# Channel products on all 128 rows, with only their tails on half-row tiles, in the last stage of a convolution and spectral-mixing kernel

## The chip, the cores and the metric

The kernel runs on one core of a Trainium2 chip. The metric is the device time of one execution in microseconds, the median over several executions; lower is better. The engines are named as the profile names them: PE (TensorE's matmuls), PEld (TensorE's weight loads), DVE (VectorE), ACT (ScalarE), POOL (GpSimd) and SP (SyncE, which here only issues transfers). A product below is one matmul together with the load of its weights.

## What is computed

The input x is 8 x 3264 x 192. First every head (24 channels) is filtered along the sequence by 7 softmaxed taps. Then 64 Fourier modes of the result are mixed by complex 192 x 192 matrices and transformed back, and a gated residual is added:

```
x   = causal 7-tap convolution of the input, taps = softmax(weight) per head
X   = rfft(x, axis=1)[:, :64]
Yr  = Xr @ w_r - Xi @ w_i;   Yi = Xr @ w_i + Xi @ w_r      (per mode)
y   = irfft(Y, n=3264, axis=1)
u   = x + y
out = u + relu(u @ w_ch)                                   (float32)
```

## The kernel before, in words

The sequence of 3264 is cut into 25 tiles of 128 positions and one half tile of 64 positions. Batches go in pairs q = 0 to 3, so a slot `xall[:, slot(q, t), i, :]` holds 128 positions x 192 channels of batch 2q + i in bf16.

**First stage.** `conv` filters a unit of 4 or 5 tiles with 64 x 64 matmuls (line 285). `dft_unit` (line 311) multiplies the tiles by the table `ftab` of cosines and sines, and `cm_bank` and `ct_bank` (lines 360, 371) transpose the filtered tiles: `cm` has the first 128 channels on the 128 rows, `ct` the last 64 channels of batch 2q on rows 0 to 63 and of batch 2q + 1 on rows 64 to 127. `mix` (line 428) multiplies the modes by the weights, which POOL loads from DRAM in 32 transfers; this is where the kernel waits for the last of them.

**Second stage**, the one that is changed. Its unit is a double tile, `duo`: two slots, so four batch tiles of 128 x 192, collected in a double PSUM bank `zt` (128 x 2 x 512 float32, four of them, `za0`, `za1`, `zb2`, `zb3`, taken in turn). The list `duos` holds 50 plain double tiles, one of the four half tiles (marked "h"), and two entries (the integers 2 and 3) at which the mixed modes of two more batches are prepared (`zw_batch`, `zw_copy`). For a double tile there are three kinds of product:

- `c`: channels by `w_ch`, 192 columns each. Per batch tile a part with the first 128 channels (`cm` and `wm`) and a part with the last 64 channels (`ct` and `wt2`, the tail).
- `g`: the inverse transform of the spectrum times `w_ch` (`ftab` and `zw`, first half), 384 columns, one per slot. After `c` and `g`, ACT applies the relu in place (line 521).
- `y`: the inverse transform of the spectrum itself (`ftab` and `zw`, second half), 384 columns, one per slot, added on top after the relu. Then `finish` adds x on DVE (line 540) into one of 7 output buffers and SP issues the transfer to DRAM (line 549, or 554 in the first four).

Before the change every product of this stage is cut into two halves of the rows: `both` (line 485) issues the product's rows 0 to 63 for one slot of the double tile and rows 64 to 127 for the other, right behind each other, as two row tiles of TensorE that run at the same time on different banks. With `first` = 0 the lower rows serve slot 0 and the upper rows slot 1; with `first` = 1 they change places. All matmuls of it are at line 499. Since two row tiles may not add into one bank at once, `turn` (line 245) puts a wait for the last matmuls of one arrangement ahead of the first matmul of the other. The order of the work is written out by hand in the loop at line 596: for entry n, `c` and `g` in the first arrangement, the second half of `y` of n - 2 and its `finish`, then `c` and `g` of n in the second arrangement, the relu, and the first half of `y` of n - 1. `first_c` (line 564) does the `c` products of the first two double tiles earlier, between the last `mix` calls.

Of the kernel before, what the change touches and what calls it, by code (L numbers as in the profile page):

```python
# [9 lines left out]
ALU = mybir.AluOpType  # L10
# [9 lines left out]
def kernel(  # L20
# [9 lines left out]
    nc = tc.nc  # L30
    B, S, D = x.shape
# [5 lines left out]
    P = 128  # L37
    NQ = B // 2
    NF = S // P
# [13 lines left out]
    def sb(name, shape, dtype, **kw):  # L53
        return pool.tile([P] + shape, dtype, tag=name, name=name, **kw)


    xall = sb("xall", [NSLOT, 2, D], BF16, align_bytes=256)
# [7 lines left out]
    cm, ct = cc[:, :, 0:CB - NT, :], cc[:, :, CB - NT:CB, :]  # L65
    ftab = sb("ftab", [NT + 1, 2 * MODES], BF16)
# [5 lines left out]
    zw = mixa[:, 0:2 * B * D].rearrange("p (b t d) -> p b t d", b=B, t=2)  # L72
    band = sb("band", [H, 2 * P], BF16)
    wm = sb("wm", [2 * D], BF16)
    w1 = sb("w1", [2 * D], BF16)
    wt2 = sb("wt2", [D], BF16)
# [54 lines left out]
    def slot(q, t):  # L131
        return NT * q + t

    def load_unit(q, t0, n, only=None):
        nf = min(n, NF - t0)
        s0 = slot(q, t0) + 1
        for i in range(2) if only is None else (only,):
# [7 lines left out]
                                           ap=[[0, P], [KK, H], [1, KK]]))  # L145
# [17 lines left out]
    for k in range(KK):  # L163
# [4 lines left out]
                            in1=wmax.unsqueeze(2).to_broadcast([P, H, KK]), op=ALU.subtract)  # L168
# [14 lines left out]
    for g in range(4):  # L183
        dst, srcv = band[32 * g:32 * g + 32, :, 32 * g:32 * g + PW], pk3[32 * g:32 * g + 32, :, :]
# [34 lines left out]
    for i in range(2):  # L219
        src = bass.AP(tensor=x.tensor, offset=x.offset + (i * S + P * NF) * D,  # L220
                      ap=[[D, HALF], [2 * S * D, NQ], [1, D]])
# [23 lines left out]
    def turn(names):  # L245

        nop = nc.tensor.nop()
        for name in names:
            tc.add_manual_dep(nop.ins, name, mybir.DependencyInfo(mybir.DependencyClass.Sync,
                                                                  mybir.DependencyReason.DATA),  # L250
                              reason="row tiles take turns on a bank")
# [144 lines left out]
    for k, u in enumerate(units):  # L396
# [5 lines left out]
        if k:  # L402
            q, t0, n = units[k - 1]
# [52 lines left out]
    some(2)  # L456


    def z_pieces(u, row, which):

        r = slice(64 * row, 64 * row + 64)
        res = []
        if u[0] == "h":
            for k, q in enumerate(u[1]):
                cols = slice(D * k, D * k + D)
                if which == "c":
                    res.append((cols, cm[r, q, 2 * NF, :], wm[r, 0:D]))
                    res.append((cols, ct[r, q, NF, :], wt2[r, :]))
                else:
                    for i in range(2):  # L470
                        res.append((cols, ftab[r, NF + i, :], zw[r, 2 * q + i, 0 if which == "g" else 1, :]))
        else:
            q, t = u
            if which == "c":
                for i in range(2):
                    res.append((slice(D * i, D * i + D), cm[r, q, 2 * t + i, :], wm[r, 0:D]))
                res.append((slice(D * row, D * row + D), ct[r, q, t, :], wt2[r, :]))
            else:
                res.append((slice(0, 2 * D), ftab[r, t, :],
                            zw[r, 2 * q:2 * q + 2, 0 if which == "g" else 1, :]))  # L480
        return res

    held = {}

    def both(duo, zt, first, which, begin=False, end=False):


        lists = (z_pieces(duo[first], 0, which), z_pieces(duo[1 - first], 1, which))
        old = held.get(id(zt))
        if old is not None and old[0] != first and not begin:  # L490
            turn(old[1])
        last = [None, None]
        for k in range(max(len(lists[0]), len(lists[1]))):
            for row in range(2):
                lst, bank = lists[row], first ^ row
                if k >= len(lst):
                    continue
                cols, l, r = lst[k]
                mm = nc.tensor.matmul(zt[:, bank, cols], l, r, start=(begin and k == 0),  # L499
                                      stop=(end and k == len(lst) - 1), skip_group_check=True)  # L500
                last[row] = mm.ins.name
        held[id(zt)] = (first, last)

    def zw_batch(b, zt, k):
        nc.tensor.matmul(zt[:, k, 0:2 * D], yet[:, 0, :, b], wm[:], start=True, stop=False)
        nc.tensor.matmul(zt[:, k, 0:2 * D], yet[:, 1, :, b], w1[:], start=False, stop=True)

    def zw_copy(b, n, src, act):
        dst = zw[:, b:b + n, :, :].rearrange("p b t d -> p b (t d)")
        if act:  # L510
            nc.scalar.activation(out=dst, in_=src, func=ACT.Copy, scale=ascale[:, 0:1])
        else:
            nc.vector.tensor_scalar(out=dst, in0=src, scalar1=ascale[:, 0:1], scalar2=None, op0=ALU.mult)

    duos = [((q, t), (q, t + 1)) for q in range(2) for t in (0, 2)]
# [4 lines left out]
    def relu(zt):  # L520
        nc.scalar.activation(out=zt[:, :, 0:2 * D], in_=zt[:, :, 0:2 * D], func=ACT.Relu)  # L521

    def finish(n):
        duo, zt = items[n]
        o = outs[n % NO]
        if duo[0][0] == "h":
            for i in range(2):
                r = slice(HALF * i, HALF * i + HALF)
                nc.vector.tensor_tensor(out=o[r, :, :].rearrange("p k (a d) -> p k a d", a=2),  # L529
                                        in0=zt[r, :, 0:2 * D].rearrange("p k (a d) -> p k a d", a=2),  # L530
                                        in1=xall[r, NF:NF + NT * (NQ - 1) + 1:NT, i, :].rearrange(
                                            "p (k a) d -> p k a d", k=2), op=ALU.add)
            for i in range(2):
                r = slice(HALF * i, HALF * i + HALF)
                dst = bass.AP(tensor=out.tensor, offset=out.offset + (i * S + P * NF) * D,
                              ap=[[D, HALF], [2 * S * D, NQ], [1, D]])
                nc.sync.dma_start(out=dst, in_=o[r, :, :].rearrange("p k (a d) -> p (k a) d", a=2))
            return
        s = [slot(*u) for u in duo]
        nc.vector.tensor_tensor(out=o[:, :, :], in0=zt[:, :, 0:2 * D],  # L540
                                in1=xall[:, s[0]:s[1] + 1:s[1] - s[0], :, :].rearrange("p k i d -> p k (i d)"),
                                op=ALU.add)
        (q0, t0), (q1, t1) = duo
        ov = o[:, :, :].rearrange("p k (i d) -> p (k i) d", i=2)
        if t0 == t1:

            dst = bass.AP(tensor=out.tensor, offset=out.offset + (2 * q0 * S + P * t0) * D,
                          ap=[[D, P], [S * D, 4], [1, D]])
            nc.sync.dma_start(out=dst, in_=ov)
        else:  # L550
            for i in range(2):
                dst = bass.AP(tensor=out.tensor, offset=out.offset + ((2 * q0 + i) * S + P * t0) * D,
                              ap=[[D, P], [P * D, 2], [1, D]])
                nc.sync.dma_start(out=dst, in_=ov[:, i:4:2, :])

    N = len(duos)
    items = [[duo, None] for duo in duos]
# [4 lines left out]
                item[1] = Z[k % 4]  # L562

    def first_c(n):
        for first in range(2):
            both(*items[n], first, "c", begin=(first == 0))

    for g in range(NG):
        mix(g)
# [23 lines left out]
    assign({k: pp.tile([P, 2, 512], F32, tag=f"zb{k}", name=f"zb{k}") for k in (2, 3)})  # L593

    ahead = 2
    for n in range(N + 2):
        duo, zt = items[n] if n < N else (None, None)
        old = [items[n - k][0] if 0 <= n - k < N else None for k in range(3)]
        zq = isinstance(duo, int)
        if n < N:  # L600
            if zq:
                for i in range(2):
                    zw_batch(2 * duo + i, zt, i)
                zw_copy(2 * duo, 2, zt[:, :, 0:2 * D], True)
            else:
                if n >= ahead:
                    both(duo, zt, 0, "c", begin=True)
                both(duo, zt, 0, "g")
        if isinstance(old[2], tuple):
            both(*items[n - 2], 1, "y", end=True)  # L610
            finish(n - 2)
        if n < N and not zq:
            if n >= ahead:
                both(duo, zt, 1, "c")
            both(duo, zt, 1, "g")
            relu(zt)
        if isinstance(old[1], tuple):
            both(*items[n - 1], 0, "y")


# [28 lines left out]
```

## Time and profile before

| what | value |
|---|---|
| median of the runs | 190.3 us (190.28, 190.3 and 192.6) |
| the profiled execution | 191.59 us, span 189.7 us |
| instructions | 6202 |
| PE, PEld, DVE, ACT, POOL busy | 154.9, 102.3, 116.5, 94.2, 66.6 us |
| moved by DMA | 40.07 MB, of which 20.05 MB written |
| matmuls of the second stage (line 499) | 33% of the span, 63 us, in the chain that ended last |

The span runs from the first to the last instruction of the profiled execution; 1.9 us of the execution's time lie outside of it. A row of the timeline or of the groups names the line, the engine, the operation, what it writes and reads, the part of TensorE's array that it uses (64\*128 is 64 rows by 128 columns), the shape of the data, and a count. The duration of a matmul is its latency; since matmuls are pipelined, what one costs is read from the distance between the starts of two neighbours, not from its duration.

### The profile page before, as it was taken

The page shows a single profiled execution, that of the slowest core. Times are in us where ns is not written, and L with a number is a line of the kernel's source. Part 1 is how long each engine was busy: PE and PEld are TensorE (multiplying, and loading weights), DVE is VectorE, ACT ScalarE, POOL GpSimd, SP SyncE. Part 2 cuts the span into 40 slices and gives each one's busy share as a digit, 9 for nine tenths or more (in the row PEclk, how much of TensorE's full clock was granted, in tenths as well). Part 3 has the DMA queues.
Part 4 walks back from the last instruction along what each step waited for, and adds up shares of the span by engine and source line. Part 5 has one row for each costly group of instructions (what it writes and reads, how often), then busy time and mean ns, then how long its engine had stood idle before and what let it go on. Part 6 is the DMA issues. An engine that isn't in the chain of part 4 may idle for free.

```text
span 189.7 us, 6202 instructions
## 1 busy us (share of the span) xinstructions
PE 154.9 (82%) x2687; PEld 102.3 (54%) x2687; DVE 116.5 (61%) x178; ACT 94.2 (50%) x129; POOL 66.6 (35%) x115
## 2 busy tenths in 40 slices
PE   0046579999999999898739749999999999999950
PEld 0023347766666756665427423666667566666620
DVE  4879555686677757464413302678575977777770
ACT  2066745545653553444523215566665666666630
POOL 7998899669557734105731000000000000000000
PEclk9999978999999999999985975999999999999997
DMA  5999999999999999995999920489986799999993
GB/s 55 147 188 189 190 173 178 191 191 192 189 190 178 178 203 207 206 207 81 199 196 205 206 46 0 152 271 363 304 274 223 225 362 323 328 325 324 327 327 133
DMA packets 63179, 40.07 MB, mean 211 GB/s; under 512 B 28848, under 2 KB 63152, under 8 KB 63152
## 3 DMA queue, kind: packets, MB, share of 16 engines
q0 software_dynamic: 36000, 19.59, 76.0%
q1 hardware_dynamic: 27152, 20.09, 31.7%
q8 instruction: 21, 0.34, 0.7%
q14 instruction: 6, 0.05, 0.1%
HBM read 39.20 MB, written 20.05 MB: 312 GB/s over the span
## 4 chain that ended last, share of the span: by engine, by line
PE 67%; DMA 13%; POOL 7%; issue 4%; DVE 4%; ACT 2%; POOLq 0%; DVEq 0%; ACTq 0%
PE zb L499 17%; PE za L499 16%; PE z L285 11%; PE low L311 9%; DMA arena<-in_moe_w_i_dram 6%; DMA arena<-in_moe_w_r_dram 4%; PE low L360 4%; POOL xall L140 4%; DMA xall<-in_x_dram 3%; PE low L371 3%; POOL arena L417 1%; PE low L324 1%; PE low L428 1%; DVE xall L305 1%; ACT za L521 1%
## 5 line engine op out<-in xcount | busy, mean ns | idle before, releaser
L285 PE MATMUL z<-xall,band 64*64 64x192 bf16 (+2 forms) x800 | 27.2, 265 | 17.5 <-DVE band L188 11.6
L140 POOL DMA_DIRECT2D xall<-in_x_dram x48 | 38.2, 810 | 7.0 <-DMA xall<-in_x_dram 5.0
L499 PEld LDWEIGHTS <-cc 64*128 64x128 bf16 x616 | 24.4, 94 | 21.2 <-PE za L499 7.3
L499 PE MATMUL za<-mixa,ftab 64*128 64x384 bf16 x208 | 32.7, 331 | 0.6 <-ACT za L521 0.3
L305 DVE CAST xall<-z 128x768 bf16<-128x768 f32 (+1 forms) x24 | 24.5, 1021 | 13.6 <-PE z L285 12.1
L540 DVE TENSOR_TENSOR arena<-za,xall 128x768 f32<-128x768 f32 x26 | 24.8, 956 | 10.8 <-PE za L499 4.5
L285 PEld LDWEIGHTS <-band 64*64 64x64 bf16 x800 | 18.1, 110 | 24.5 <-ACT band L186 12.0
L499 PE MATMUL zb<-mixa,ftab 64*128 64x384 bf16 (+1 forms) x224 | 31.2, 311 | 0.1
L303 ACT CAST xall<-z 128x768 bf16<-128x768 f32 (+1 forms) x24 | 20.4, 851 | 15.1 <-PE z L285 13.8
L540 DVE TENSOR_TENSOR arena<-zb,xall 128x768 f32<-128x768 f32 x24 | 22.9, 957 | 7.5 <-ACT za L521 4.0
L521 ACT ACTIVATE za<-za 128x768 f32<-128x768 f32 x26 | 20.7, 795 | 11.1 <-PE za L499 11.1
L521 ACT ACTIVATE zb<-zb 128x768 f32<-128x768 f32 x25 | 19.9, 795 | 12.3 <-PE zb L499 12.3
L499 PEld LDWEIGHTS <-ftab 64*128 64x128 bf16 x432 | 19.6, 94 | 4.2 <-issue 2.1
L311 PE MATMUL low<-xall,ftab 128*128 128x384 bf16 x100 | 21.6, 343 | 0.0
L499 PE MATMUL za<-wm,cc 64*128 64x192 bf16 x208 | 17.4, 245 | 0.2
L499 PE MATMUL zb<-wm,cc 64*128 64x192 bf16 x200 | 17.1, 248 | 0.4 <-DVE arena L529 0.3
L360 PEld LDWEIGHTS <-xall 128*128 128x128 bf16 x208 | 14.0, 103 | 3.2 <-issue 0.5
L340 DVE COPY cc<-low 128x1024 bf16<-128x1024 bf16 (+2 forms) x19 | 11.8, 620 | 4.4 <-PE low L360 2.3
L340 DVE COPY cc<-r 128x1024 bf16<-128x1024 bf16 (+2 forms) x10 | 6.0, 604 | 13.7 <-PE r L371 8.3
L338 ACT COPY cc<-low 128x1024 bf16<-128x1024 bf16 (+1 forms) x9 | 8.5, 941 | 11.4 <-PE low L371 5.1
L417 POOL DMA_DIRECT2D arena<-in_moe_w_r_dram x12 | 7.6, 632 | 17.1 <-PE low L428 10.4
L499 PE MATMUL za<-wt,cc 64*128 64x192 bf16 x104 | 12.8, 243 | 0.0
(104 smaller groups left out, 175.0 us busy)
## 6 DMA issues: line engine op xcount, KB each, us to landing
out_dram<-arena SPq DMA_DIRECT2D x46, 384.0 KB, 3.9
xall<-in_x_dram POOLq DMA_DIRECT2D x24, 192.0 KB, 8.1
xall<-in_x_dram POOLq DMA_DIRECT2D x16, 240.0 KB, 7.1
arena<-in_moe_w_r_dram POOLq DMA_DIRECT2D x12, 288.0 KB, 11.1
arena<-in_moe_w_i_dram POOLq DMA_DIRECT2D x12, 288.0 KB, 11.2
out_dram<-arena SPq DMA_DIRECT2D x10, 192.0 KB, 2.9
xall<-in_x_dram POOLq DMA_DIRECT2D x8, 144.0 KB, 7.0
cc<-in_moe_w_r_dram POOLq DMA_DIRECT2D x4, 288.0 KB, 7.2
```

Source lines behind the costliest of these rows:

```text
L140: nc.gpsimd.dma_start(out=xall[:, s0:s0 + nf, i, :], in_=src)
L285: mm = nc.tensor.matmul(ov[c], band[r, h, c.start + shift + 64 * (r is UP and c is LO): c.start + shift + 64 * (r is UP and c is LO) + 64] ...
L303: nc.scalar.copy(out=dst, in_=srcv)
L305: nc.vector.tensor_copy(out=dst, in_=srcv)
L311: nc.tensor.matmul(xp, ftab[:, t, :], xall[:, slot(q, t), :, :], start=(t == 0), stop=False, skip_group_check=True)
L338: nc.scalar.copy(out=out, in_=in_)
L340: nc.vector.tensor_copy(out=out, in_=in_)
L360: nc.tensor.transpose(tp[:, P * k:P * k + P], xall[:, slot(q, t), i, 0:P], ident[:])
L417: nc.gpsimd.dma_start(out=wbuf(g)[64 * half:64 * half + 64, :, :, :], in_=src[4 * g:4 * g + 4, :, :].rearrange("m (p j) e -> p m j e", j=3))
L499: mm = nc.tensor.matmul(zt[:, bank, cols], l, r, start=(begin and k == 0), stop=(end and k == len(lst) - 1), skip_group_check=True)
L521: nc.scalar.activation(out=zt[:, :, 0:2 * D], in_=zt[:, :, 0:2 * D], func=ACT.Relu)
L540: nc.vector.tensor_tensor(out=o[:, :, :], in0=zt[:, :, 0:2 * D], in1=xall[:, s[0]:s[1] + 1:s[1] - s[0], :, :].rearrange("p k i d -> p k (i ...
```

## The change

`both` and `z_pieces` are replaced by three functions, and the loop by another order:

- `heads(n)`: the parts of `c` with the first 128 channels, four products per double tile, each on all 128 rows.
- `tails(n, first)`: the parts with the last 64 channels, in two turns. In a turn two half-row products run at the same time on the two banks; `first` tells which rows serve which slot. The second turn begins with a wait for the first. For the half tiles ("h") the tails are four products on all rows, in the first turn alone (the rows of the other batch are zero there).
- `modes(n, which)`: `g` (`which` = 0) or `y` (`which` = 1), two products of 384 columns on all 128 rows.

```
+    def tails(n, first):
+        duo, zt = items[n]
+        if duo[0][0] == "h":
...
+            return
+        if first:
+            turn(order[n])
+        names = []
+        for row in range(2):
+            bank = row ^ first
+            q, t = duo[bank]
+            r = slice(64 * row, 64 * row + 64)
+            mm = nc.tensor.matmul(zt[:, bank, D * row:D * row + D], ct[r, q, t, :], wt2[r, :], start=(first == 0),
+                                  stop=False, skip_group_check=True)
+            names.append(mm.ins.name)
+        order[n] = names
+
+    def heads(n):
+        duo, zt = items[n]
+        turn(order[n])
+        for k, u in enumerate(duo):
+            for j in range(2):
+                cols = slice(D * j, D * j + D)
+                product(n, k, cols, cm[:, u[1][j], 2 * NF, :] if u[0] == "h" else cm[:, u[0], 2 * u[1] + j, :],
+                        wm[:, 0:D])
+
+    def modes(n, which):
...
+                q, t = u
+                product(n, k, slice(0, 2 * D), ftab[:, t, :], zw[:, 2 * q:2 * q + 2, which, :], stop=(which == 1))
```

The loop, new order:

```
+    for n in range(N + 2):
+        if tiles(n):
+            if n > ahead and n - 1 < N and not tiles(n - 1):
+                tails(n, 0)
+            if n >= ahead:
+                tails(n, 1)
...
+        if tiles(n - 2) and n >= 2:
+            modes(n - 2, 1)
             finish(n - 2)
+        if tiles(n):
             if n >= ahead:
+                heads(n)
+            if tiles(n + 1) and n + 1 >= ahead:
+                tails(n + 1, 0)
+            modes(n, 0)
+            relu(items[n][1])
```

`first_c` becomes `tails(n, 0)`, `tails(n, 1)`, `heads(n)`. In `finish` the last double tile is added and stored in two halves, the first by SP's queue, the second by ACT's:

```
+        if n == N - 1:
+            for k, (q, t) in enumerate(duo):
+                nc.vector.tensor_tensor(out=o[:, k, :], in0=zt[:, k, 0:2 * D],
+                                        in1=xall[:, s[k], :, :].rearrange("p i d -> p (i d)"), op=ALU.add)
...
+                eng = nc.scalar if k else nc.sync
+                eng.dma_start(out=dst, in_=o[:, k, :].rearrange("p (i d) -> p i d", i=2))
+            return
```

On PE, before, in the middle of a double tile (here `za0`): the last two products of its first arrangement, the `y` half of the double tile two earlier (`zb2`), and the beginning of the second arrangement. `zw` lies in the tensor that the listing calls mixa, and "waits PE" marks a turn.

```order
L499 LDWEIGHTS ftab_61
L499 MATMUL za0_2054<-mixa_63,ftab_61 128x384
L499 LDWEIGHTS ftab_61
L499 MATMUL za0_2054<-mixa_63,ftab_61 128x384
L499 LDWEIGHTS ftab_61 [waits PE_49]
L499 MATMUL zb2_2135<-mixa_63,ftab_61 128x384
L499 LDWEIGHTS ftab_61
L499 MATMUL zb2_2135<-mixa_63,ftab_61 128x384
L499 LDWEIGHTS cc_60 [waits PE_49]
L499 MATMUL za0_2054<-wm_65,cc_60 128x192
```

Between the products that the second turn waits for (`g` on `za0`) and the turn lies one pair of half-row products (`y` on `zb2`), and all products use half of the rows.

On PE, after, around the two turns of a double tile's tails (here `zb2`): the end of `g` of the double tile before (`za1`), the second turn of the tails (line 481, half of the rows), `y` of the double tile two earlier (`za0`, line 462, all rows), and the first of the heads.

```order
L462 LDWEIGHTS ftab_61
L462 MATMUL za1_2055<-mixa_63,ftab_61 128x384
L481 LDWEIGHTS cc_60 [waits PE_49]
L481 MATMUL zb2_2129<-wt2_67,cc_60 128x192
L481 LDWEIGHTS cc_60
L481 MATMUL zb2_2129<-wt2_67,cc_60 128x192
L462 LDWEIGHTS ftab_61
L462 MATMUL za0_2054<-mixa_63,ftab_61 128x384 [waits Activation_49]
L462 LDWEIGHTS ftab_61
L462 MATMUL za0_2054<-mixa_63,ftab_61 128x384
L462 LDWEIGHTS cc_60 [waits PE_49]
L462 MATMUL zb2_2129<-wm_65,cc_60 128x192
```

Between the two turns of the tails, and between the second turn and the heads, now stand two products of 384 columns on all rows. A plain double tile has 12 products (four on half of the rows, in two pairs, and eight on all rows) where it had 20 on half of the rows (in ten pairs). In the whole loop the listing has 188 places at which half-row and full-row products follow each other; before it had 5.

On SP, the transfers to DRAM (the difference of the two listings, "-" before, "+" after):

```order
-L549 DMA out_dram<-arena 128x4x192 x16
-L537 DMA out_dram<-arena 64x4x192 x2
-L549 DMA out_dram<-arena 128x4x192 x30
-L644 UNCONDITIONAL_BRANCH
+L567 DMA out_dram<-arena 128x2x192 x8
+L562 DMA out_dram<-arena 128x4x192 x16
+L540 DMA out_dram<-arena 64x4x192 x2
+L562 DMA out_dram<-arena 128x4x192 x29
+L551 DMA out_dram<-arena 128x2x192
```

One transfer of a whole double tile became one of half a double tile here; the other half stands at the end of ACT's list, behind the last relu.

More of the change, by code (lines that the diff above doesn't have):

```diff
@@ L456 @@
     some(2)
[L459 to L469, printed above, removed]
-                    for i in range(2):
[L471 to L477, printed above, removed]
-            else:
-                res.append((slice(0, 2 * D), ftab[r, t, :],
-                            zw[r, 2 * q:2 * q + 2, 0 if which == "g" else 1, :]))
-        return res
@@ L483 @@
[L483 to L502, printed above, removed]
+    order = {}
@@ new lines, in product @@
+    def product(n, bank, cols, l, r, start=False, stop=False):
+        mm = nc.tensor.matmul(items[n][1][:, bank, cols], l, r, start=start, stop=stop, skip_group_check=True)
+        return mm.ins.name
+    def tails(n, first):
+        duo, zt = items[n]
+        if duo[0][0] == "h":
+            if first == 0:
+                order[n] = [product(n, k, slice(D * j, D * j + D), ct[:, q, NF, :], wt2[:, :], start=(j == 0))
+                            for k, u in enumerate(duo) for j, q in enumerate(u[1])]
+            return
[10 more added lines that the diff above has]
+        order[n] = names
@@ new lines, in heads @@
+    def heads(n):
[7 more added lines that the diff above has]
+    def modes(n, which):
+        duo, zt = items[n]
+        for k, u in enumerate(duo):
+            if u[0] == "h":
+                for j, q in enumerate(u[1]):
+                    for i in range(2):
+                        product(n, k, slice(D * j, D * j + D), ftab[:, NF + i, :], zw[:, 2 * q + i, which, :],
+                                stop=(which == 1 and i == 1))
+            else:
+                q, t = u
+                product(n, k, slice(0, 2 * D), ftab[:, t, :], zw[:, 2 * q:2 * q + 2, which, :], stop=(which == 1))
@@ L539, in finish @@
         s = [slot(*u) for u in duo]
+        if n == N - 1:
+            for k, (q, t) in enumerate(duo):
+                nc.vector.tensor_tensor(out=o[:, k, :], in0=zt[:, k, 0:2 * D],
+                                        in1=xall[:, s[k], :, :].rearrange("p i d -> p (i d)"), op=ALU.add)
+                dst = bass.AP(tensor=out.tensor, offset=out.offset + (2 * q * S + P * t) * D,
+                              ap=[[D, P], [S * D, 2], [1, D]])
+                eng = nc.scalar if k else nc.sync
+                eng.dma_start(out=dst, in_=o[:, k, :].rearrange("p (i d) -> p i d", i=2))
+            return
         nc.vector.tensor_tensor(out=o[:, :, :], in0=zt[:, :, 0:2 * D],
@@ L564, in first_c @@
     def first_c(n):
-        for first in range(2):
-            both(*items[n], first, "c", begin=(first == 0))
+        tails(n, 0)
+        tails(n, 1)
+        heads(n)
     for g in range(NG):
@@ L595, with tiles @@
     ahead = 2
+    def tiles(n):
+        return n < N and isinstance(duos[n], tuple)
     for n in range(N + 2):
[L597 to L610, printed above, removed]
+        if tiles(n):
+            if n > ahead and n - 1 < N and not tiles(n - 1):
+                tails(n, 0)
+            if n >= ahead:
+                tails(n, 1)
+        elif n < N:
+            zt = items[n][1]
+            for i in range(2):
+                zw_batch(2 * duos[n] + i, zt, i)
+            zw_copy(2 * duos[n], 2, zt[:, :, 0:2 * D], True)
+        if tiles(n - 2) and n >= 2:
+            modes(n - 2, 1)
             finish(n - 2)
-        if n < N and not zq:
+        if tiles(n):
             if n >= ahead:
[L614 to L618, printed above, removed]
+                heads(n)
+            if tiles(n + 1) and n + 1 >= ahead:
+                tails(n + 1, 0)
+            modes(n, 0)
+            relu(items[n][1])
 _INS = ['x', 'weight', 'moe_w_r', 'moe_w_i', 'moe_w_ch']
```

## The prediction

> **What bounds the kernel now.** I read the stages by engine first (start and end, length, then busy time and count of PE, PEld, DVE, ACT and POOL, the granted clock, the DMA share, GB/s).
>
> ```profile
> 80.00:98.00 18.00, 13.65 (x279) 9.85 (x279) 7.32 (x19) 7.07 (x15) 7.35 (x12) 1.00 1.03 169
> ...
> 118.70:140.00 21.30, 21.24 (x339) 13.72 (x336) 15.22 (x17) 13.62 (x17) 0.00 (x0) 1.00 0.81 271
> 140.00:150.00 10.00, 9.64 (x161) 6.64 (x157) 6.82 (x8) 5.67 (x7) 0.00 (x0) 1.00 0.72 234
> 150.00:180.00 30.00, 30.00 (x494) 19.71 (x492) 23.56 (x25) 19.71 (x25) 0.00 (x0) 1.00 0.99 328
> ```
>
> The changed stage runs from about 116 us to the end. Two resources look full in it: PE is busy for 30.00 of 30 us, and the DMA share is 0.99. Which one sets the pace is seen in the waits and in the rate by the moment (GB/s in 40 slices of 150 to 180 us):
>
> ```profile
> SPq L549 <- DVE arena L540: 34.1, 44, 2.3
> ```
>
> ```profile
> GB/s 231 295 340 370 373 366 373 373 327 363 294 243 294 371 370 355 297 372 304 283 347 174 359 367 352 373 307 344 331 298 372 287 309 360 301 375 299 301 373 308
> ```
>
> SP's queue waits for the results, 34.1 us in all, not the results for the queue; and the transfers reach 373 GB/s in many slices and fall below 300 in others. At 373 GB/s a double tile of 393 KB needs 1.05 us. What it takes is read from PE's timeline:
>
> ```profile
> 164.08 0.34 PE L499 MATMUL zb<-wm,cc 64*128 64x192 bf16 x4
> 164.26 0.24 PE L499 MATMUL zb<-wt,cc 64*128 64x192 bf16 x2
> 164.34 0.33 PE L499 MATMUL zb<-mixa,ftab 64*128 64x384 bf16 x2
> 164.50 0.33 PE L499 MATMUL za<-mixa,ftab 64*128 64x384 bf16 x2
> 164.66 0.33 PE L499 MATMUL zb<-wm,cc 64*128 64x192 bf16 x4
> 164.83 0.25 PE L499 MATMUL zb<-wt,cc 64*128 64x192 bf16 x2
> 164.91 0.33 PE L499 MATMUL zb<-mixa,ftab 64*128 64x384 bf16 x2
> 165.07 0.33 PE L499 MATMUL za<-mixa,ftab 64*128 64x384 bf16 x2
> 165.30 0.34 PE L499 MATMUL zb<-wm,cc 64*128 64x192 bf16 x4
> ```
>
> ```profile
> 165.30 0.20 PEld L499 LDWEIGHTS <-cc 64*128 64x128 bf16 x6 [0.29 <-PE zb L499]
> ```
>
> From 164.08 to 165.30 is one double tile: 1.22 us. A pair of half-row products ("x2") costs 0.16 us with 384 columns (164.34 to 164.50) and 0.08 with 192 (164.26 to 164.34); four and six pairs make 4 x 0.1625 + 6 x 0.082 = 1.14 us. The other 0.08 is the turn: 165.07 plus 0.16 would be 165.23, but the next product starts at 165.30, its weights waiting for PE's own products on zb, and the first product after a wait loses another 0.01 (164.08 to 164.26 against 164.66 to 164.83). DVE and ACT follow with room to spare:
>
> ```profile
> L540 DVE TENSOR_TENSOR arena<-za,xall 128x768 f32<-128x768 f32 x5 | 4.8, 958 | 1.3 <-ACT za L521 0.8 <-ACT zb L521 0.5
> ...
> L521 ACT ACTIVATE zb<-zb 128x768 f32<-128x768 f32 x5 | 4.0, 795 | 2.1 <-PE zb L499 2.1
> ```
>
> So PE sets the pace, and the stage is priced by the distance between starts of matmuls.
>
> **The change, part by part.** *Products.* Twenty half-row products in ten pairs become four half-row ones in two pairs and eight full ones. What does a full product cost? The first stage has them: the transform (line 311, 384 columns) and the transposes (line 360, 128 columns).
>
> ```profile
> 38.00 0.81 PE L311 MATMUL low<-xall,ftab 128*128 128x384 bf16 x4
> 38.65 0.61 PE L360 MATMUL low<-ident,xall 128*128 128x128 bf16 x8
> 39.19 0.41 PE L371 MATMUL low<-ident,xall 128*64 128x128 bf16 x8
> ```
>
> Four in 0.65 us: 0.1625 each, the same as a pair, with new weights for each. By columns, 192 cost 0.082. So ten slots cost 1.14 us after as before: by itself this removes nothing, only instructions on a queue that was not late.
>
> *Turns.* The second turn of the tails and the heads each wait for the tail pair before. What a wait without cover costs is seen where the first double tiles are begun:
>
> ```profile
> 107.27 0.24 PE L499 MATMUL za<-wt,cc 64*128 64x192 bf16 x2
> 107.58 0.34 PE L499 MATMUL za<-wm,cc 64*128 64x192 bf16 x4
> ```
>
> 0.31 us from a pair to the product that waits for it. Now two products of 384 columns stand between, 0.08 + 2 x 0.1625 = 0.41 us, so the wait is over in time. Saved: 0.08 us on 46 double tiles, 3.7 us. (Behind the two zw entries three waits stay open, as they do now.) If the cover failed, 0.08 would come back and no more.
>
> *Changes of shape.* This is what I hold to be decisive. All products of the stage used 64\*128; now the order goes half rows, full, half rows, full in every double tile: four changes each, 188 in the loop against 5. The trace of before has such places:
>
> ```profile
> 43.15 0.65 PE L311 MATMUL low<-xall,ftab 128*128 128x384 bf16 x3
> 43.73 0.30 PE L371 MATMUL low<-ident,xall 128*64 128x128 bf16 x4
> ```
>
> ```profile
> 139.98 0.49 PE L499 MATMUL zb<-mixa,ftab 64*128 64x384 bf16 x4
> 140.40 0.38 PE L505 MATMUL za<-wm,yet 128*128 128x384 bf16 x1
> 140.62 0.33 PE L506 MATMUL za<-w,yet 128*128 128x384 bf16 x1
> 140.78 0.33 PE L505 MATMUL za<-wm,yet 128*128 128x384 bf16 x1
> 140.95 0.33 PE L506 MATMUL za<-w,yet 128*128 128x384 bf16 x1
> 141.21 0.50 PE L499 MATMUL zb<-mixa,ftab 64*128 64x384 bf16 x4
> ```
>
> ```profile
> 140.40 0.14 PEld L505 LDWEIGHTS <-yet 128*128 128x128 bf16 x1 [0.32 <-issue]
> ```
>
> The three transforms at 43.15 take 0.58 us to the next start; two of them cost 0.325, so the last, ahead of another shape, costs 0.255: 0.0925 too much. From 139.98 the two pairs should be through at 140.305; the first full product starts at 140.40, 0.095 late, and its weight load, which waited for nothing that the trace shows, starts no earlier. Back to half rows: 140.95 + 0.1625 = 141.11, but 141.21, 0.0975 late. With the shape unchanged (38.00 to 38.65, one kind of product to another) nothing is lost. So both directions between just these two shapes cost 0.095, and the first product behind one is 0.01 longer, as behind a wait: I take 0.105 (bounds 0.0925 without the 0.01, 0.1075 with both at their highest). In all 183 x 0.105 = 19.2 us.
>
> The Trainium skill says the same of the cause: in "TensorEngine Tiling (Array Packing)", Key Properties, changing the tiling mode, not just the tile, drains TensorE. It has no price there; "TensorE: Matmul & The Clock Gate", Step-by-step: what each phase is for, lets a drain last about 128 cycles, an estimate of 0.053 us at 2.4 GHz, by which the sum below would end at 195.5 us. The trace agrees on the cause and shows 0.095.
>
> *Where the time goes then.* A double tile takes 1.14 + 4 x 0.105 = 1.56 us. Relu (0.795) and the add (0.958) have more room than now, transfers need 1.05 of 1.56 us, so nothing else becomes late. The two more changes in `first_c` lie ahead of the last `mix`, where PE waits for weights:
>
> ```profile
> 111.36 0.46 PE L428 MATMUL low<-arena,mixa 128*16 128x192 bf16 x12 [1.58 <-DMA arena<-in_moe_w_i_dram]
> ```
>
> *The end.* The last add becomes two of 384 columns, and the second half's transfer goes out on ACT's queue, behind its last relu, which is long done.
>
> ```profile
> 114.17 0.62 DVE L513 TENSOR_SCALAR mixa<-low,ascale 128x384 bf16<-128x384 f32 x1 [1.05 <-PE low L588]
> ```
>
> ```profile
> out_dram<-arena SPq DMA_DIRECT2D x46, 384.0 KB, 3.9
> ...
> out_dram<-arena SPq DMA_DIRECT2D x10, 192.0 KB, 2.9
> ```
>
> Two adds cost between 0.96 (half of 0.958 each) and 1.24 us (the nearest row with 384 columns, 0.62), so the second half is ready up to 0.28 later, and lands in 2.9 us instead of 3.9. I take -0.8 us, near the transfers' rows (bounds -1.0 and 0, if two transfers side by side are no faster than one).
>
> *Sum.* +19.2 - 3.7 - 0.8 = +14.7 us. On the profiled execution, 191.6 us, this makes 206.3; the median of the runs is 190.3, 1.3 below it, so I forecast **205.0 us**. By the bounds: 183 x 0.0925 - 3.7 - 1.0 = +12.2 (202.5), and 183 x 0.1075 - 3.4 (turns at 0.075) - 0 = +16.3 (206.6).
>
> **The rivals.** *The change of shape costs nothing here*, since the weights for the other rows could be loaded while the last product of the other shape runs. Then the double tile takes 1.14 us, and the time is 190.3 - 3.7 - 0.8 = 185.8 us: faster. Transfers would just allow it (1.05). The point from which this side decides is a price of 4.5 / 183 = 0.025 us per change. For it speaks only that both shapes never alternated so often; against it both directions in the rows above. 0.06.
>
> *The transfers set the pace behind that*: with free changes of shape, but output at the 328 GB/s of 150 to 180 us, a double tile stays at 1.2 us, and only the end gains: 189.5 us, no difference. For it: the DMA share of 0.99; against it the 373 GB/s and SP's 34.1 us of waiting. 0.04.
>
> *Only one direction costs*: 92 changes, 9.7 - 4.5 = +5.2, 195.5 us, slower. Against it: 0.095 one way and 0.0975 the other, though the second row has a turn in it too. 0.03.
>
> *Full-row weights are not loaded behind the product before.* Eight loads a double tile would then be paid in full:
>
> ```profile
> L311 PEld LDWEIGHTS <-ftab x100: 95/98/152, 17.4 to 78.9; 128*128 128x128 bf16 x100
> ```
>
> At 0.098 us, 8 x 0.098 x 48 = 38 us more, 243 us. The four transforms in 0.65 us exclude it: with paid loads they would take 1.04. The Trainium skill says so in "TensorE: Matmul & The Clock Gate", The mechanism: a load overlaps running matmuls only where the row group differs. The trace disagrees. 0.02.
>
> **How the numbers follow.** The forecast has 0.85, its rivals 0.06, 0.04, 0.03 and 0.02. Slower by over 2% (about what a measurement of this kernel can tell from no change; 194.1 us) are the forecast, the one direction and the paid loads: 0.90. Within 2%: 0.04. Faster: 0.06. The forecast's bounds are 202.5 and 206.6; with the spread of the runs before (the shown ones reach 2.3 us apart) I give 200.5 to 208.0, which leaves out about two in ten with the rivals.
>
> **What would show it.** In the changed profile a steady double tile should take 1.56 us between the starts of its heads; each change of shape a gap of about 0.095 us ahead of a weight load that waits for nothing; no idle time put down to PE itself at the turns; a DMA share near 0.76 at about 250 GB/s; a granted clock of 1.00, since from 80 to 98 us, with PE busy for 13.65 of 18 us, it was 1.00 as well. The last transfer should land about 2.9 us after its issue. The prediction is wrong if the period is below 1.3 us, if the gaps are there in one direction only, or if the time grows at another place than between 118 us and the end.

## The result, and the profile after

The changed kernel takes 205.19 us (median of four runs, 203.03 to 205.9), the kernel before beside it 190.84 us: 1.0716 times as long, with a 95% interval of 1.0604 to 1.0828. (A ratio with an interval, here and below, is worked out over the executions; it is not the quotient of the two medians, which is 1.075 here.) The forecast was 205.0 us. The profiled execution took 205.9 us, its span 204.1 us, 14.4 more than before.

The stages by engine, after (same columns as in the prediction):

```profile
118.70:140.00 21.30, 21.19 (x162) 10.80 (x160) 13.40 (x14) 11.03 (x15) 0.00 (x0) 1.00 0.67 224
140.00:150.00 10.00, 9.91 (x81) 5.99 (x82) 4.78 (x5) 5.60 (x8) 0.00 (x0) 1.00 0.73 245
150.00:180.00 30.00, 29.81 (x232) 15.14 (x230) 18.88 (x20) 14.89 (x19) 0.00 (x0) 1.00 0.72 238
```

PE still counts as busy all the time, at a granted clock of 1.00, with less than half of the matmuls (232 instead of 494 in 30 us) and 238 GB/s where there were 328. A busy share near one tells nothing here; the distance between starts does. PE's timeline of one double tile, from the first turn of the tails to the next one's:

```profile
165.36 0.26 PE L481 MATMUL za<-wt,cc 64*128 64x192 bf16 x2
165.54 0.50 PE L462 MATMUL za<-mixa,ftab 128*128 128x384 bf16 x2
165.98 0.26 PE L481 MATMUL za<-wt,cc 64*128 64x192 bf16 x2
166.16 0.50 PE L462 MATMUL zb<-mixa,ftab 128*128 128x384 bf16 x2
166.50 0.49 PE L462 MATMUL za<-wm,cc 128*128 128x192 bf16 x4
166.93 0.26 PE L481 MATMUL zb<-wt,cc 64*128 64x192 bf16 x2
```

165.36 to 166.93 is 1.57 us. A tail pair takes 0.18 to the next start instead of 0.08 (165.36 to 165.54 and 165.98 to 166.16); two products of 384 columns take 0.44 ahead of half rows (165.54 to 165.98) but 0.34 ahead of more full rows (166.16 to 166.50); four heads take 0.43 ahead of half rows where 0.33 would do. Four times about 0.1, one at each change of shape. The weight loads of the same stretch:

```profile
165.35 0.10 PEld L481 LDWEIGHTS <-cc 64*128 64x128 bf16 x2 [0.16 <-issue]
165.54 0.11 PEld L462 LDWEIGHTS <-ftab 128*128 128x128 bf16 x2
165.97 0.10 PEld L481 LDWEIGHTS <-cc 64*128 64x128 bf16 x2 [0.32 <-PE za L481]
166.16 0.11 PEld L462 LDWEIGHTS <-ftab 128*128 128x128 bf16 x2
166.34 0.43 PEld L462 LDWEIGHTS <-cc 128*128 128x128 bf16 x4
```

The load at 165.35 waited for nothing that the trace shows; the one at 165.97, the second turn, is put down to PE's own products on za. Whether that is a wait or only a name is what one experiment below decides.

The stage can be bounded by its adds on DVE. The first and the last of the kernel before, then of the changed one:

```profile
119.23 0.96 DVE L540 TENSOR_TENSOR arena<-za,xall 128x768 f32<-128x768 f32 x1 [3.20 <-PE za L499]
```

```profile
183.49 0.96 DVE L540 TENSOR_TENSOR arena<-za,xall 128x768 f32<-128x768 f32 x1
```

```profile
119.07 0.96 DVE L553 TENSOR_TENSOR arena<-za,xall 128x768 f32<-128x768 f32 x1 [2.40 <-PE za L462]
```

```profile
198.61 1.02 DVE L546 TENSOR_TENSOR arena<-za,xall 128x384 f32<-128x384 f32 x2
```

From the first to the last, 64.26 us became 79.54: +15.28. Ahead of the first it is 0.16 us less, and from the last one's start to the end of the span 6.19 (189.68 - 183.49) became 5.52 (204.13 - 198.61): -0.67. Together +14.4 us: all of the loss lies in the steady loop.

### The profile page after: what moved, and what is told of

It is laid out like the page before. It is cut to its first block, busy times and chain, and to the rows that moved or that the text cites. A ratio compares the mean times of both kernels' runs of the same rounds, so it can differ in the third digit from the quotient of the medians.

```text
span 204.1 us, 5359 instructions
## 1 busy us (share of the span) xinstructions
PE 170.8 (84%) x2263; PEld 102.0 (50%) x2263; DVE 116.9 (57%) x179; ACT 94.0 (46%) x129; POOL 66.9 (33%) x115
## 4 chain that ended last, share of the span: by engine, by line
PE 72%; DMA 9%; DVE 7%; issue 4%; ACT 4%; POOL 2%; DVEq 0%; POOLq 0%; ACTq 0%
PE za L462 15%; PE zb L462 15%; PE z L285 11%; DMA arena<-in_moe_w_i_dram 9%; PE low L311 9%; PE zb L481 5%; PE za L481 4%; PE low L360 4%; PE low L371 3%; DVE arena L180 2%; PE low L428 1%; PE low L324 1%; DVE xall L305 1%; POOL xall L140 1%; POOL arena L417 1%
## 5 line engine op out<-in xcount | busy, mean ns | idle before, releaser
L553 DVE TENSOR_TENSOR arena<-za,xall 128x768 f32<-128x768 f32 x25 | 23.9, 958 | 17.3 <-PE za L462 16.9
L524 ACT ACTIVATE za<-za 128x768 f32<-128x768 f32 x26 | 20.7, 795 | 19.3 <-PE za L462 19.2
L462 PE MATMUL za<-mixa,ftab 128*128 128x384 bf16 x104 | 26.6, 338 | 0.6 <-ACT za L524 0.6
L462 PE MATMUL zb<-mixa,ftab 128*128 128x384 bf16 (+1 forms) x112 | 25.6, 319 | 0.0
L481 PEld LDWEIGHTS <-cc 64*128 64x128 bf16 x200 | 9.7, 92 | 24.4 <-issue 8.0
L462 PEld LDWEIGHTS <-cc 128*128 128x128 bf16 x208 | 18.5, 98 | 6.8 <-PE za L481 0.7
L462 PEld LDWEIGHTS <-ftab 128*128 128x128 bf16 x216 | 13.4, 98 | 10.2 <-issue 1.3
L360 PEld LDWEIGHTS <-xall 128*128 128x128 bf16 x208 | 14.7, 107 | 3.2 <-issue 0.5
L481 PE MATMUL za<-wt,cc 64*128 64x192 bf16 x104 | 13.3, 253 | 0.2
L462 PE MATMUL za<-wm,cc 128*128 128x192 bf16 x104 | 12.9, 246 | 0.2
```

The source lines that it names most:

```text
L360: nc.tensor.transpose(tp[:, P * k:P * k + P], xall[:, slot(q, t), i, 0:P], ident[:])
L462: mm = nc.tensor.matmul(items[n][1][:, bank, cols], l, r, start=start, stop=stop, skip_group_check=True)
L481: mm = nc.tensor.matmul(zt[:, bank, D * row:D * row + D], ct[r, q, t, :], wt2[r, :], start=(first == 0), stop=False, skip_group_check=True)
```

## The experiments

The theory is that of the prediction: each change between half-row and full-row products costs PE about 0.105 us. Rival 1: products on all rows cost more than their columns, because of their weight loads. Rival 2: PE's waits for its own products, two per double tile now, cost the time, as the name at 165.97 suggests. The end of the program was tested by itself. "Per double tile" is the median distance between the starts of neighbouring adds on DVE in the steady loop; it is 1.570 us for the changed kernel and 1.22 for the kernel before.

**Tails on all rows too** (no change of shape, no wait):

```
-        if first:
-            turn(order[n])
...
-            mm = nc.tensor.matmul(zt[:, bank, D * row:D * row + D], ct[r, q, t, :], wt2[r, :], start=(first == 0),
-                                  stop=False, skip_group_check=True)
+        if first == 0:
+            for k, (q, t) in enumerate(duo):
+                product(n, k, slice(0, 2 * D), ct[:, q, t, :], wtb[:, :], start=True)
...
     def heads(n):
         duo, zt = items[n]
-        turn(order[n])
```

Here `wtb` holds the tail of `w_ch` twice, as a block diagonal of 128 x 384.

> The changed kernel with the tails on all 128 rows too: one product of 384 columns per slot, with a block-diagonal weight tile, in place of the two turns of half-row pairs. No change of shape is left in the steady loop and no wait of PE for itself; it pays 0.16 us per double tile for columns that multiply zeros. Theory (a change of shape costs 0.105 us): a double tile takes 1.14 + 0.16 = 1.30 us instead of 1.57, and the time is about 194 us, 11 below the changed kernel and 3 above the kernel before. Rival 1 (products on all rows cost more than their columns, since their weights are not loaded behind the product before): all ten products have that cost now, the double tile stays at 1.57 us or above, 205 us or more. Rival 2 (the waits of PE for its own products): 194 us as well, since they are gone too.

Measured: 192.22 us, before beside it 190.34, ratio 1.0117 (1.006 to 1.0174). PE's timeline:

```profile
168.93 0.49 PE L465 MATMUL zb<-wtb,cc 128*128 128x384 bf16 x2
169.25 0.81 PE L465 MATMUL za<-mixa,ftab 128*128 128x384 bf16 x4
169.91 0.49 PE L465 MATMUL zb<-wm,cc 128*128 128x192 bf16 x4
170.24 0.33 PE L465 MATMUL zb<-wtb,cc 128*128 128x384 bf16 x1
```

From 168.93 to 170.24 it is 1.305 us per double tile: two tails (0.32), four products of modes (0.66) and four heads (0.33), all at the price of their columns. Rival 1 is out: ten products on all rows, each with its own weights, lose nothing. Without the 0.1625 of the columns that multiply zeros, 1.14 us are left, as the prediction had it. The time came out lower than the 194 us expected, though: from the first add to the last 67.89 us pass, 3.63 more than before, but in this profiled execution the first add came 1.88 us earlier, and from the last add to the end 4.91 us passed where it was 6.19. No run was made to explain these two.

**Two changes of shape instead of four:**

```
             if n >= ahead:
                 tails(n, 1)
+            if tiles(n + 1) and n + 1 >= ahead:
+                tails(n + 1, 0)
+            if n >= ahead:
+                heads(n)
+            modes(n, 0)
+            relu(items[n][1])
...
-        if tiles(n - 2) and n >= 2:
-            modes(n - 2, 1)
-            finish(n - 2)
...
+        if tiles(n - 1) and n >= 1:
+            modes(n - 1, 1)
+            finish(n - 1)
```

> The changed kernel with the second turn of a double tile's tails and the first turn of the next one's right behind each other, so that there are two changes of shape per double tile instead of four; y is done one double tile later instead of two. The products and the number of waits are the same. Theory: 1.14 + 2 x 0.105 = 1.35 us, and about 0.04 more since the heads now wait behind 0.26 us only: 1.39 us per double tile, 198 us. Rival 1 (products on all rows): 1.57 us, 205 us. Rival 2 (the waits): two per double tile as before, with less between them: 1.57 us or more, 205 us or more.

Measured: 198.45 us, ratio 1.0419 (1.0379 to 1.046), 1.408 us per double tile.

```profile
169.04 0.34 PE L481 MATMUL zb<-wt,cc 64*128 64x192 bf16 x4
169.36 0.50 PE L462 MATMUL zb<-wm,cc 128*128 128x192 bf16 x4
169.70 0.49 PE L462 MATMUL zb<-mixa,ftab 128*128 128x384 bf16 x2
170.02 0.49 PE L462 MATMUL za<-mixa,ftab 128*128 128x384 bf16 x2
170.44 0.26 PE L481 MATMUL zb<-wt,cc 64*128 64x192 bf16 x2
```

Between `g` and `y`, both on all rows, 0.32 us pass for two products (169.70 to 170.02); between `y` and the tails 0.42 (170.02 to 170.44). The two pairs from 169.04 take 0.32 to the heads: 0.16 by their columns, 0.1 for the change, and 0.05 more. These 0.05 are most likely the wait of the heads for the second turn, which the prediction read as 0.31 us from a pair to the product that waits for it, where only 0.26 us (two pairs and a change) lie between here; no run takes this wait out. The same products and as many waits, but 0.16 us less per double tile than with four changes.

**Four changes of shape, no wait:**

```
-        if first:
-            turn(order[n])
         names = []
-        for row in range(2):
+        for row in range(1):
...
     def heads(n):
         duo, zt = items[n]
-        turn(order[n])
```

> The changed kernel with only the lower half-row product of each turn of the tails (the tail of the other batch is left out), so that no two row tiles run at once and PE never waits for its own products. Columns and the four changes of shape per double tile stay, since a pair costs as much as one of its halves. Theory: 1.57 us per double tile, 205 us as the changed kernel. Rival 2 (the waits): 1.14 to 1.2 us per double tile, 186 to 189 us. Rival 1 (products on all rows): 205 us.

Measured: 204.04 us, ratio 1.0707 (1.0651 to 1.0764), 1.563 us per double tile. The waits, longest in total (engine, line waited for: us in total, times, longest), of the changed kernel and of this one:

```profile
PEld L481 <- issue: 8.0, 49, 0.3
PEld L481 <- PE za L481: 8.0, 26, 0.3
...
PEld L481 <- PE zb L481: 7.5, 23, 0.6
```

```profile
PEld L479 <- issue: 22.5, 93, 0.6
```

Without any turn the loads of the tails stand idle as long, 22.5 us against 8.0 + 8.0 + 7.5 = 23.5, but now all of it has no releaser. Rival 2 is out: the changed kernel's 15.5 us "waiting for PE" were a semaphore that had come in before it was needed, at a place where PE stood anyway.

**Two changes of shape and an open wait:**

```
-            if n > ahead and n - 1 < N and not tiles(n - 1):
+            if n >= ahead:
                 tails(n, 0)
-            if n >= ahead:
                 tails(n, 1)
...
-            if tiles(n + 1) and n + 1 >= ahead:
-                tails(n + 1, 0)
             modes(n, 0)
```

> The changed kernel with both turns of the tails right behind each other, as a block of half-row products: two changes of shape per double tile instead of four, but nothing between the first turn and the second that waits for it (0.31 us from one to the other where 0.08 would do). Theory: 1.14 + 2 x 0.105 + 0.22 = 1.57 us per double tile, by chance the same as the changed kernel: 205 us, but the trace shows the time at another place, ahead of the second turn. Rival 2 (the waits are all of the cost): an open wait costs more than a covered one, 215 us or more. Rival 1 (products on all rows): 1.57 + 0.22 us, 215 us.

Measured: four executions between 204.17 and 207.91 us, beside 190.34. They lie too far apart to tell this kernel from the changed one by its time, but all are well below the 215 us that either rival gives. The profiled one shows 1.597 us per double tile, 0.03 above the changed kernel. The weight loads:

```profile
168.25 0.10 PEld L481 LDWEIGHTS <-cc 64*128 64x128 bf16 x2 [0.32 <-issue]
168.57 0.10 PEld L481 LDWEIGHTS <-cc 64*128 64x128 bf16 x2 [0.23 <-PE zb L481]
168.76 0.11 PEld L462 LDWEIGHTS <-ftab 128*128 128x128 bf16 x2
```

From 168.25 to 168.57 passes a real wait for a turn: 0.32 us from one pair's loads to the next's. So a wait without cover costs 0.24 us, about as much as two changes of shape (0.21), and 1.14 + 0.21 + 0.24 make 1.59, the measured period. Hiding the wait by an alternating order that adds two changes only trades the one for the other.

**The end alone**, on the kernel before:

```
+        if n == N - 1:
+            for k, (q, t) in enumerate(duo):
...
+                eng = nc.scalar if k else nc.sync
```

> The kernel before with nothing but the last double tile added and stored in two halves, the second on ACT's queue. Theory: the span from the start of the last add to the end of the program falls from 6.19 to about 5.5 us, as in the changed kernel (5.47), so the time falls by 0.7 us, 0.4%. Rival (the end gained only because the transfers were less crowded in the changed kernel, where one landed in 2.5 us instead of 3.9): no gain, 0 to 0.2 us.

Measured: 191.5 us beside 190.2, ratio 1.0043 (1.0005 to 1.0081): no gain, if anything a loss. From the start of the last add to the end 6.48 us pass, where it was 6.19 (and 5.52 in the changed kernel, where the expectation has 5.47). GB/s of the transfers in 40 slices from 183 to 190 us, of the kernel before and of this one:

```profile
GB/s 373 369 364 369 373 377 373 360 373 373 369 373 377 369 360 377 373 369 373 377 123 26 26 22 22 22 26 22 13 0 0 0 0 0 0 0 0 0 0 0
```

```profile
GB/s 364 360 373 377 364 364 373 386 355 377 377 364 360 377 386 355 377 373 369 360 373 373 369 360 88 22 22 26 22 22 22 26 4 0 0 0 0 0 0 0
```

In both the transfers run at about 370 GB/s nearly to the end, and then a rest of 22 to 26 GB/s, a sixteenth of the rate, follows for 1.4 us. Since the rate is full before the last half is handed over, an earlier first half most likely only queues earlier.

**The end undone**, on the changed kernel (the block above taken out), with the changed kernel once more beside it:

> The changed kernel with the last double tile added and stored whole again, on SP's queue, as before the change. Theory of the prediction (the split itself saves 0.7 us): the span from the start of the last add to the end rises from 5.5 to about 6.2 us, the time by 0.7 us, 0.35%, above the changed kernel run beside it. Rival, after the end alone gained nothing on the kernel before (the queue to DRAM is less full in the changed kernel, a transfer lands in 2.5 us instead of 3.9, and that is the gain): the span stays at 5.5 us or falls to 5.0, the time is the same within 0.3 us or lower.

> The changed kernel once more, unchanged, so that its end and its time stand beside the kernel with the end undone on the same chip: 205 us, 1.57 us per double tile, 5.5 us from the start of the last add to the end.

Measured: 204.49 us without the split (ratio 1.0733, 1.0677 to 1.0789), 205.71 us with it (1.0777, 1.0723 to 1.0832). The intervals overlap. From the start of the last add to the end both take 5.92 us, neither the 6.2 of the theory nor the 5.5 of the rival, and both have 79.54 us from the first to the last add and 1.570 us per double tile; the profiled executions differ ahead of the first add (at 117.1 and 118.6 us). So the split saves nothing measurable in either kernel. What shortened the end of the changed kernel in its first profiled execution is not shown. Its transfers are less crowded: one lands in 2.5 us (median of 45) where it was 3.9.

```profile
out_dram<-arena SPq DMA_DIRECT2D x45, 384.0 KB, 2.5
```

But in the changed kernel too the last transfers run at about 370 GB/s, and its end differs from one execution to the next. GB/s in 40 slices from 197 to 204 us, of the changed kernel (5.52 us from the last add to the end) and of its second profiled execution (5.92):

```profile
GB/s 347 334 364 342 347 272 13 9 136 369 369 382 369 369 365 373 373 377 369 373 360 373 373 360 369 382 303 40 22 22 26 0 0 0 0 0 0 0 0 0
```

```profile
GB/s 342 351 290 18 9 9 9 13 22 26 320 369 334 355 377 373 360 364 382 377 364 377 356 377 369 373 364 373 193 22 13 0 0 0 0 0 0 0 0 0
```

The rest lasts about 0.7 us in the one and 0.35 in the other, against 1.4 before the change, and the longer rest belongs to the shorter end. So 0.4 us of the end is the difference between two executions of one kernel, and one profile of each kernel cannot place the 0.67.

## Why the prediction was right, step by step

- **What bounds the stage.** Right: PE, by the distance of the starts. After the change PE alone sets it, at a granted clock of 1.00 as forecast: the DMA share fell from 0.99 to 0.72 (0.76 was forecast) and the rate to 238 GB/s (about 250). That the transfers did not set the pace before rests on SP's 34.1 us of waiting and on rates of 370 GB/s elsewhere in the stage; no version ran below 1.22 us per double tile, so how far they would allow it is not shown.
- **Price of the products.** Right: ten slots of columns make 1.14 us, and the kernel with all products on all rows shows 1.305 with 0.1625 of extra columns in it.
- **Changes of shape.** Right, in cause and size. By the kernels with none and with four, (1.570 - 1.1425) / 4 = 0.107 us each, against 0.105 taken and 0.1075 as upper bound; the kernel with four changes and no wait gives 0.105. Two changes give 1.1425 + 0.214 = 1.356, and the 0.05 told above make up the measured 1.408. Both directions cost: two products of 384 columns take 0.44 instead of 0.34 ahead of half rows, a pair 0.18 instead of 0.08 ahead of full rows. One of the rows it was read from was read short: from 140.40 to 140.62 the first full product takes 0.22, 0.06 more than its columns and not 0.01; this does not come back in the changed loop (two products in 0.34 from 166.16), so the 0.01 was the right size. The Trainium skill's rule, that changing the tiling mode drains TensorE ("TensorEngine Tiling (Array Packing)", Key Properties), agrees; the estimate from the 128 cycles of the Trainium skill's "TensorE: Matmul & The Clock Gate", Step-by-step: what each phase is for, 0.053 us, is half of the measured price. What happens inside PE at a change these runs do not separate. The load and the matmul behind it start late together (165.35 and 165.36), which speaks for a pause ahead of both and against a load that merely takes its own 0.10 us in the open.
- **The covered turns.** Right in size: with the cover, the waits cost no more than 0.007 us (1.570 against 1.563 without them), so the 0.08 are saved (1.22 to 1.14), and 0.24 are lost where the wait is left open. One sign was read wrongly ahead: I wrote that no idle time would be put down to PE at the turns, but the profile put 15.5 us down to it. The kernel without turns shows that this time belongs to the changes of shape.
- **The end.** Here the step failed: "-0.8 us", for two adds and two queues. The end did shorten, by 0.67 us in the profiled execution and 0.27 in the other one (5.92 against 6.19), but not by the split, which on the kernel before gives no gain and whose removal from the changed one loses none. The two adds took 1.02 us, within the 0.96 to 1.24 forecast; the term that failed is the landing. I took 2.9 us for half a double tile against 3.9 for a whole one. The last half landed after 4.1 us in the kernel before with the split, after 3.1 and 3.5 in the changed one's two executions, and the last two whole ones after 3.5 (median) with the end undone. The 2.9 is the median of transfers in the first half of the stage, and both medians seem to hold queueing: the same rows read 2.5 and 2.0 us when the double tiles come slower. Why the end of the changed kernel is shorter stays open.
- **The sum.** 19.2 - 3.7 = +15.5 for the loop against +15.28 measured; -0.8 for the end against -0.67, not by the split; -0.16 ahead of the first add was not forecast. So the loop came out by its cause, and the last few tenths by luck: the executions of the changed kernel alone lie 2.9 us apart, and the kernel before took 190.84 us beside it where the sum began at 190.3.

No version tried is faster than the kernel before; the one with block-diagonal tails comes nearest of those without its turn, 1.2% longer. The 0.08 us per double tile that the turn costs is less than what any order tried here pays to avoid it: one change of shape already costs 0.107, and the block-diagonal tails cost 0.1625 in columns.

## What to carry to other kernels

Count the places at which neighbouring matmuls use the array in different shapes before halving or doubling rows: at a granted clock of 1.00 each cost 0.107 us here, more than a pair of half-row products of 192 columns (0.08). Where part of a contraction is short, compare that with keeping one shape throughout, all half rows or all full rows with zeros (1.22 and 1.305 us per double tile here, against 1.408 with two changes and 1.570 with four). If another shape is needed, group its products, but not so that one of them has to wait for another: the group with an open wait was no faster than the alternating order. The price of such a place could be read off an earlier stage of the same trace here, from the distance between starts, with a stretch of unchanged shape beside it as the control.

## What the runs showed that was not expected

- A releaser named by the profile can be one that had come in before it was needed: 8.0 and 7.5 us put down to PE's own products turned into 22.5 us without a releaser when there was nothing left to wait for, at the same period (1.570 and 1.563 us).
- With output at about 370 GB/s nearly to the last, a sixteenth of the rate (22 to 26 GB/s) goes on for 1.4 us in the kernel before after the rest is done. The share of one sixteenth makes it look like one of the 16 DMA engines being late, but no view here shows the engines one by one. With all tails on all rows this slow rest was absent (GB/s in 40 slices from 183 to 190 us below), and 4.91 us passed from the last add to the end where it was 6.19. Its cause was not tested.

```profile
GB/s 382 369 369 158 101 369 373 364 377 377 290 40 285 373 373 373 377 373 299 364 373 382 364 373 365 377 364 365 369 377 233 4 0 0 0 0 0 0 0 0
```
